# Late loads in larger pieces, a wider output projection and ScalarE centring in a one-core decode block

## The chip, the cores and the metric

The kernel runs on one core of a Trainium2 chip. The metric is the device time of one execution in microseconds (us). TensorE (PE, with its weight loads as PEld), VectorE (DVE), ScalarE (ACT), GpSimd (POOL) and SyncE (SP) are the engines. SP issues nearly all loads; each load is spread over the core's sixteen DMA engines. Every DMA engine works off its share of a queue in order; such a share is called a ring here.

## The reference, cut to what matters

One token (width 512) passes through an attention layer with a cache and then through a small network, with residual additions. x, weights and caches are bf16.

```python
h  = x  + A(layernorm(x))            # attention: 32 query heads, 8 cache heads, 16384 keys, head size 128
h2 = h  + B(layernorm(h))
# A: q = x @ wq; p = softmax(q k^T / sqrt(128)); o = p v; return o(4096) @ wo(4096 x 512)
# B: one token, so the spatial shifts leave nothing of w1, w2:
#    return x + gelu(layernorm(x) @ w3(512 x 1792)) @ w4(1792 x 512)
```

For a sequence of one the shifted slices in B are all padding, so w1 and w2 drop out, and the kernel does not load them. What has to come from memory is 79 MB: the two caches (32 MiB each), wq and wo (4 MiB each), w3 and w4 (1.75 MiB each).

## The kernel before, in words

The program is written as a list of operations per engine. A small planner, `Program.op`, is told what tiles each operation reads and writes, and puts a semaphore wait where another engine or a load has to come first; within an engine the order is that of the source. A load has a semaphore of its own, and an operation that reads a piece of a buffer waits for the load of that piece (`("r", y, n)` are the pieces of key buffer y, `("v", n)` those of the value buffer).

The eight cache heads are taken as four pairs, `j` from 0 to 3. For each pair there are two halves of the keys, loaded into kb[0] and kb[1] (4 MiB each), and the values, loaded into vb (8 MiB). DVE transposes a key half in eight steps into kt (L393), PE makes the scores (L401, 32 products a half in groups of four), and the load of the next pair's half is issued as soon as the transposes have freed the buffer. Then follow the softmax (L412 to L431: a maximum, two small products to spread it, the exponential on ACT, two transposes into pt on DVE, a product that adds up the denominators into one column of A_ps), the values products (L439: sixteen groups of four, each group filling four strips of 32 output rows with 512 columns), and `gather` (L450 to L458), which sums the wanted blocks on DVE and places them in A_ps by one float32 product (L456).

The value load of a pair is issued when the values products of the pair before are done. For pairs 0 to 2 it is one load of 8 MiB. For the last pair it is cut by V3 into the first three quarters and the last quarter, and the products of groups 12 to 15 alone wait for the last quarter.

After the last pair the buffers of keys are used for weights: wo goes into kb[0], as two loads (WO: row blocks 0 to 23 and 24 to 31; a row block is 128 partitions of 512 columns), w3 and w4 into kb[1], w3 as two loads (three of four row blocks, then one) and w4 as four (6, 4, 3 and 1 of 14 row blocks). They are all issued on SP in that order, behind the last value load.

The end of the kernel runs so: DVE takes the reciprocal of the denominators (L484), scales and sums A_ps into the attention output o_b, 128 partitions by 32 columns (L485 to L490). PE adds x by a small product (L491) and then the output projection (L496): for each of 32 row blocks four products of 128 columns, one for each quarter q of the 512 outputs, into strip q of O_ps[0], so that the result lies as 4 strips of 128. `row_sums` (L264 to L275) copies this to hr with its sum, squares it, transposes it to hT, and gets mean and mean square by a float32 product with mean4 (L273). DVE subtracts the mean from the transposed columns (hc, L505). PE multiplies by w3 (L511, sixteen products of 448 columns). The variance and the inverse root (three Newton steps) run on DVE beside it, and once more on POOL for the residual branch, which ends in xsum (L521). ACT applies gelu with the inverse root as its scale (L524, two halves), DVE transposes to hcol (L528), PE multiplies by w4 (L535, four products for each of 14 row blocks), DVE adds xsum (fin, L539), SP stores.

`spin(n)` (L253) puts n products of 128x512 into PE's order, whose result nobody reads.

Of the kernel before, what the change touches and what calls it, by code (L numbers as in the profile page):

```python
# [109 lines left out]
D = 512  # L110
# [6 lines left out]
NCH = D // 128  # L117
FQ = FM // 4
NHC = FM // 128
WO = ((0, 24), (24, 32))  # L120
W3 = ((0, 3), (3, 4))
W4 = ((0, 6), (6, 10), (10, 13), (13, 14))
PAIRS = HKV // 2
V3 = ((0, 3), (3, 4))
RPARTS = 6
QPAD = 4 * 7
QW = QPAD + 128
# [4 lines left out]
def bass_sequential_preLN__gqa_block_cached__mixer_s_mlp__decode_kernel(  # L132
# [13 lines left out]
    with ExitStack() as ctx:  # L146
# [40 lines left out]
        p_sb = sb("p_sb", [128, 1024], BF16)  # L187
        pt = sb("pt", [128, 32, 2, 2, 16], BF16)
        od = sb("od", [128, 128], FP32)
        den = sb("den", [128, 1], FP32)  # L190
        o_m = sb("o_m", [128, 4, 32], FP32)
        o_f = sb("o_f", [128, 32], FP32)
# [27 lines left out]
        def pair_rows(src, j):  # L220
            return src[0, 2 * j:2 * j + 2].rearrange("g (u t) d -> (g u) (t d)", u=64)
# [4 lines left out]
                 also=[("r", y, i) for i in range(1, RPARTS)])  # L226

        def load_values(j):
            src = pair_rows(A_v_cache, j)
            if j < PAIRS - 1:  # L230
                load("v", vb[:, :], src, ("v", 0), also=[("v", 1)])
            else:
                n = 64 * DH
                for i, (lo, hi) in enumerate(V3):
                    load(f"v3{i}", vb[:, lo * n:hi * n], src[:, lo * n:hi * n], ("v", i))


        def dve(fn, r=(), w=(), bank=()):
# [38 lines left out]
        def variance(i):  # L277

            s, S = st[i], ("st", i)

            dve(lambda e: e.scalar_tensor_tensor(s[:, 2:3], s[:, 0:1], s[:, 0:1], s[:, 1:2],
                                                 ALU.mult, ALU.subtract), r=[(S, 0)], w=[(S, 2)])
# [19 lines left out]
        def inverse_root(i, n, by):  # L302
# [7 lines left out]
            for k in range(3):  # L310
# [6 lines left out]


        load("x4", x4[:, :], A_x[0, 0:1, :].rearrange("o (q j) -> (o q) j", q=4), "x4", "ACT")
        load("wq", wq_sb[:, 0:NCH * HQ * DH], A_wq.rearrange("(p k) c -> p (k c)", k=NCH), ("v", 0))  # L320
        load_keys(0, 0)
        load_keys(0, 1)

        dve(lambda e: e.memset(mean4[:, :], 1.0 / (32 * D)), w=["mean4"])
        dve(lambda e: e.memset(ident_f[:, :], 0.0), w=["ident_f"])
        P.op("POOL", lambda e: e.affine_select(out=ident_f[:, :], in_=ident_f[:, :], pattern=[[-1, 128]],  # L326
                                               compare_op=ALU.not_equal, fill=1.0, base=0,
# [10 lines left out]
        seeds(0, (0,))  # L338
        inverse_root(0, 0, dve)
        dve(lambda e: e.tensor_scalar(xn[:, :], hT[:, :, 0], st[0][:, 0:1], st[0][:, 6:7],  # L340
                                      ALU.subtract, ALU.mult),
            r=["hT", (("st", 0), 0), (("st", 0), 6)], w=["xn"])


# [25 lines left out]
        for j, (row, key) in enumerate(rows):  # L370
            for k in range(NCH):
                for g in range(2):
                    at = k * HQ * DH + (2 * j + g) * REP * DH
                    pe(lambda e, row=row, k=k, g=g, at=at: e.matmul(  # L374
                        row[64 * g:64 * g + 64, :], copies(xn[:, k:k + 1], 64), wq_sb[:, at:at + REP * DH],
                        start=(k == 0), stop=(k == NCH - 1)), r=["xn", ("v", 0)], w=[key], bank=[key])
# [32 lines left out]
        def softmax(j):  # L409

            s_all = s_ps[:, :, :].rearrange("p y f -> p (y f)")
            dve(lambda e: e.tensor_reduce(mx[:, :], s_all, AX.X, ALU.max), r=[("s", 0), ("s", 1)], w=["mx"], **both)  # L412
            pe(lambda e: e.matmul(m_ps[0:1, 0:128], mx[:, :], ident_f[:, :], start=True, stop=True),  # L413
               r=["mx", "ident_f"], w=["m"], bank=["mn"])
            dve(lambda e: e.tensor_reduce(nm[:, :, :], m_ps[0:1, 0:128].rearrange("o (g n h) -> o g h n", g=2, h=REP),
                                          AX.X, ALU.max), r=["m"], w=["nm"], bank=["mn"])
            pe(lambda e: e.matmul(n_ps[:, 0:2 * REP], nscale[0:1, :], nm[:, :, :].rearrange("o g h -> o (g h)"),
                                  start=True, stop=True), r=["nm", "nscale"], w=["n"], bank=["mn"])
            dve(lambda e: e.scalar_tensor_tensor(nmh[:, :], n_ps[:, 0:2 * REP], 1.0,  # L419
                                                 maskgh[:, :, :].rearrange("p g h -> p (g h)"), ALU.mult, ALU.mult,  # L420
                                                 accum_out=bias[:, :]), r=["n", "maskgh"], w=["nmh", "bias"],
                bank=["mn"])
            act(lambda e: e.activation(p_sb[:, :], s_all, ACTF.Exp, bias=bias[:, 0:1], scale=float(SCALE),  # L423
                                       accum_out=acc[:, :]),
                r=[("s", 0), ("s", 1), "bias"], w=["p", "acc"], **both)
            for g in range(2):
                dve(lambda e, g=g: e.transpose(pt[64 * g:64 * g + 64, :, :, g, :], p_sb[64 * g:64 * g + 64, :]),  # L427
                    r=["p"], w=["pt"])
            pe(lambda e: e.matmul(A_ps[:, 128:129], zd[:, 96 - 32 * j:224 - 32 * j], acc[:, :],  # L429
                                  start=(j == 0), stop=(j == PAIRS - 1), skip_group_check=True),  # L430
               r=["acc", "zd"], w=["A"], bank=["A"])  # L431

        def values(j):
            tiles = vb[:, :].rearrange("p (x c l d) -> p x l c d", x=4, c=8, l=8)
            for q in range(16):
                for ct in range(4):
                    xl, ch = 2 * q + ct // 2, ct % 2
                    parts = [int(xl // 8 >= V3[1][0])] if j == PAIRS - 1 else [0, 1]
                    pe(lambda e, q=q, ct=ct, xl=xl, ch=ch: e.matmul(  # L439
                        O_ps[j % 2][32 * ct:32 * ct + 32, :], pt[:, xl, ch, :, :].rearrange("p g u -> p (g u)"),  # L440
                        tiles[:, xl // 8, xl % 8, 4 * ch:4 * ch + 4, :], start=(q == 0), stop=(q == 15)),
                       r=[("v", n) for n in parts] + ["pt"], w=[("O", j % 2)], bank=[("O", j % 2)])

        def gather(j):

# [24 lines left out]
            if j < PAIRS - 1:  # L470
                load_values(j + 1)
        act(lambda e: e.activation(scr[0:1, 1:2], mean4[0:1, 0:1], ACTF.Gelu_apprx_tanh), r=["mean4"], w=["scr"])
        for n, (lo, hi) in enumerate(WO):
            load(f"wo{n}", wo_sb[:, lo * D:hi * D], A_wo.rearrange("(p r) c -> p (r c)", p=128)[:, lo * D:hi * D],
                 ("r", 0, n))
        w3_in = B_w3.rearrange("(p k) f -> p k f", p=128)
        for n, (lo, hi) in enumerate(W3):
            load(f"w3{n}", w3_sb[:, lo:hi, :], w3_in[:, lo:hi, :], ("r", 1, n))
# [11 lines left out]
        dve(lambda e: e.tensor_copy(o_b[:, :], o_f[:, :]), r=["o_f"], w=["o_b"])  # L490
        pe(lambda e: e.matmul(O_ps[0][:, 0:128], quarter[:, :, :].rearrange("p q u -> p (q u)"), x4[:, :],  # L491
                              start=True, stop=False, skip_group_check=True),
           r=["quarter", "x4"], w=[("O", 0)], bank=[("O", 0)])
        for r_ in range(32):
            for q in range(4):
                pe(lambda e, r_=r_, q=q: e.matmul(O_ps[0][32 * q:32 * q + 32, 0:128], copies(o_b[:, r_:r_ + 1], 32),  # L496
                                                  wo_sb[:, r_ * D + q * 128:r_ * D + (q + 1) * 128],
                                                  start=False, stop=(r_ == 31), skip_group_check=True),
                   r=["o_b", ("r", 0, piece(WO, r_))], w=[("O", 0)], bank=[("O", 0)])
# [16 lines left out]
        seeds(1, (0, 1))  # L516
        inverse_root(1, 1, dve)
        inverse_root(1, 0, pool)
        pool(lambda e: e.tensor_scalar(xs[:, :], hr[:, :], s[:, 0:1], s[:, 6:7], ALU.subtract, ALU.mult),
            r=["hr", (S, 0), (S, 6)], w=["xs"])  # L520
        pool(lambda e: e.tensor_tensor(xsum[:, :], hr[:, :], xs[:, :], ALU.add), r=["hr", "xs"], w=["xsum"])  # L521
        for n in range(2):
# [6 lines left out]
                hcol[:, lo:hi, :].rearrange("p m u -> p (m u)"),  # L529
                hg[:, :].rearrange("p (i m) -> p m i", m=NHC)[:, lo:hi, :]), r=[("hg", n)], w=[("hcol", n)])  # L530
        for m in range(NHC):
            if m in (W4[1][0], W4[2][0]):
                spin(1)
            for o in range(4):
                pe(lambda e, m=m, o=o: e.matmul(  # L535
                    n_ps[32 * o:32 * o + 32, 0:128], hcol[:, m, :], w4_sb[:, m, o * 128:(o + 1) * 128],
# [38 lines left out]
```

## Time and profile before

| | us |
|---|---|
| median of 3 runs (lowest to highest) | 192.22 (192.14 to 192.45) |
| the profiled execution, its own time | 192.01 |
| its span | 190.7 |
| PE busy, DVE busy, ACT busy, POOL busy | 117.2, 114.8, 8.7, 7.7 |
| DMA: mean rate over the span | 416 GB/s |
| packets' time of the main queue, share of sixteen DMA engines' span | 97.1% |

The page gives for each engine its busy share of the span; for the DMA queues the packets, megabytes and the share of the sixteen engines' time; the chain of work that ended last, followed backwards through what released each step; and groups of instructions by source line with their mean duration and the idle time before them, with what ended it. The timeline shows instructions in order of time: start, length, engine, line, output and inputs, and in brackets the idle time of that engine before it and its releaser. The windows view gives, for stretches of time, the busy time of an engine and the TensorE clock that was granted (1.00 is full speed). The trace also holds each DMA packet with its start, length and size, and the moment at which each of a load's sixteen parts reported its completion.

### The profile page before, as it was taken

The page shows a single profiled execution, that of the slowest core. Times are in us where ns is not written, and L with a number is a line of the kernel's source. Part 1 is how long each engine was busy: PE and PEld are TensorE (multiplying, and loading weights), DVE is VectorE, ACT ScalarE, POOL GpSimd, SP SyncE. Part 2 cuts the span into 40 slices and gives each one's busy share as a digit, 9 for nine tenths or more (in the row PEclk, how much of TensorE's full clock was granted, in tenths as well). Part 3 has the DMA queues.
Part 4 walks back from the last instruction along what each step waited for, and adds up shares of the span by engine and source line. Part 5 has one row for each costly group of instructions (what it writes and reads, how often), then busy time and mean ns, then how long its engine had stood idle before and what let it go on. Part 6 is the DMA issues. An engine that isn't in the chain of part 4 may idle for free.

```text
span 190.7 us, 1877 instructions
## 1 busy us (share of the span) xinstructions
PE 117.2 (61%) x797; PEld 45.6 (24%) x799; DVE 114.8 (60%) x176; ACT 8.7 (5%) x14; POOL 7.7 (4%) x16
## 2 busy tenths in 40 slices
PE   0129098793085598951754979605739996293793
PEld 0114033221031142211221322202213321141632
DVE  7755597984402898945026989550169896605171
ACT  3000000002000000001000000020000000500010
POOL 7100000000000000000000000000000000000052
PEclk9999969999558589995597899975665999659699
DMA  6999999999999999998999999979999998999991
GB/s 227 433 440 440 440 440 442 440 440 430 433 419 426 433 488 440 430 426 351 440 440 440 529 440 430 426 344 412 433 426 423 464 478 351 416 436 406 421 397 62
DMA packets 3191, 79.28 MB, mean 416 GB/s; under 512 B 368, under 2 KB 496, under 8 KB 1008
## 3 DMA queue, kind: packets, MB, share of 16 engines
q1 hardware_dynamic: 3176, 79.17, 97.1%
q8 instruction: 6, 0.10, 0.2%
q14 instruction: 1, 0.01, 0.0%
q10 hardware_dynamic: 8, 0.00, 0.0%
HBM read 79.17 MB, written 0.00 MB: 415 GB/s over the span
## 4 chain that ended last, share of the span: by engine, by line
DMA 77%; DVE 19%; SPq 1%; issue 0%; PE 0%
DMA kb<-in_A_k_cache_dram 63%; DVE kt L393 19%; DMA kb<-in_B_w_dram 14%; SPq L218 1%; PE mn_ps L535 0%; DVE fin L539 0%; SPq L101 0%
## 5 line engine op out<-in xcount | busy, mean ns | idle before, releaser
L401 PE MATMUL s_ps<-kt,qb 128*128 128x512 bf16 x256 | 70.0, 416 | 19.1 <-DVE kt L393 16.6
L393 DVE STREAM_TRANSPOSE kt<-kb 128x1024 int32<-128x1024 int32 x64 | 73.0, 1210 | 11.6 <-DMA kb<-in_A_k_cache_dram 11.6
L401 PEld LDWEIGHTS s_ps<-kt,qb 128*128 128x128 bf16 x256 | 23.3, 104 | 64.8 <-DVE kt L393 38.8
L439 PE MATMUL O_ps<-vb,pt 128*32 128x512 bf16 x256 | 23.6, 550 | 16.8 <-DMA vb<-in_A_v_cache_dram 14.7
L450 DVE TENSOR_SCALAR od<-O_ps,rowc 128x128 f32<-128x128 f32 x4 | 1.4, 351 | 32.7 <-PE O_ps L439 32.7
L439 PEld LDWEIGHTS O_ps<-vb,pt 128*32 128x32 bf16 x256 | 8.9, 132 | 29.9 <-DMA vb<-in_A_v_cache_dram 15.0
L427 DVE STREAM_TRANSPOSE pt<-p_sb 64x1024 bf16<-64x1024 bf16 x8 | 9.9, 1239 | 5.4 <-ACT p_sb L423 5.3
L423 ACT ACTIVATE p_sb<-s_ps,bias 128x1024 bf16<-128x1024 f32 x4 | 4.5, 1114 | 156.7 <-DVE nmh L419 156.7
L412 DVE TENSOR_REDUCE mx<-s_ps 128x1 f32<-128x1024 f32 x4 | 4.9, 1225 | 4.5 <-PE s_ps L401 4.5
L309 POOL TENSOR_SCALAR st<-st 128x1 f32<-128x1 f32 x1 | 0.3, 265 | 177.2 <-DVE st L294 177.2
L374 PE MATMUL O_ps<-vb,xn 128*64 128x512 bf16 x16 | 3.6, 632 | 5.5 <-DMA vb<-in_A_wq_dram 5.5
L456 PE MATMUL A_ps<-od,zo 128*128 128x128 f32 x8 | 2.0, 326 | 6.5 <-DVE od L453 6.5
L429 PE MATMUL A_ps<-acc,zd 128*128 128x1 f32 x8 | 1.9, 311 | 6.3 <-ACT p_sb L423 6.3
L496 PE MATMUL O_ps<-kb,o_b 128*32 128x128 bf16 x128 | 3.3, 282 | 2.4 <-DMA kb<-in_A_wo_dram 2.4
L413 PE MATMUL mn_ps<-ident_f,mx 128*1 128x128 f32 x8 | 1.5, 271 | 5.3 <-DVE mx L412 5.3
L453 DVE SCALAR_TENSOR_TENSOR od<-O_ps,rowc,od 128x128 f32<-128x128 f32 x12 | 4.2, 351 | 0.4
L256 PE MATMUL O_ps<-p_sb,pt 128*128 128x512 bf16 x15 | 4.0, 388 | 0.3 <-issue 0.3
L331 DVE CAST ident<-ident_f 4x4 bf16<-4x4 f32 x1 | 3.8, 3849 | 0.6 <-POOL ident_f L326 0.6
L334 PE MATMUL O_ps<-x,quarter 4*128 4x128 bf16 x1 | 0.3, 282 | 5.8 <-DVE quarter L332 5.8
L378 DVE STREAM_TRANSPOSE qcol<-O_ps 128x256 f32<-128x256 f32 x4 | 1.6, 428 | 3.6 <-PE O_ps L374 3.6
L267 DVE TENSOR_SCALAR_CACHE_REDUCE hr<-O_ps 128x128 f32<-128x128 f32 x2 | 0.6, 292 | 5.1 <-PE O_ps L496 4.7
L496 PEld LDWEIGHTS O_ps<-kb,o_b 128*32 128x32 bf16 x128 | 2.8, 127 | 2.8 <-issue 2.4
(76 smaller groups left out, 47.8 us busy)
## 6 DMA issues: line engine op xcount, KB each, us to landing
kb<-in_A_k_cache_dram SPq DMA_DIRECT2D x8, 4096.0 KB, 29.6
vb<-in_A_v_cache_dram SPq DMA_DIRECT2D x1, 6144.0 KB, 27.3
vb<-in_A_wq_dram SPq DMA_DIRECT2D x1, 4096.0 KB, 12.1
kb<-in_A_wo_dram SPq DMA_DIRECT2D x1, 3072.0 KB, 27.3
vb<-in_A_v_cache_dram SPq DMA_DIRECT2D x1, 2048.0 KB, 31.8
kb<-in_B_w_dram SPq DMA_DIRECT2D x1, 1344.0 KB, 23.6
kb<-in_A_wo_dram SPq DMA_DIRECT2D x1, 1024.0 KB, 29.4
kb<-in_B_w_dram SPq DMA_DIRECT2D x1, 768.0 KB, 25.6
```

The source lines that it names most:

```text
L256: pe(lambda e: e.matmul(O_ps[1][:, :], pt[:, 0:2, :, :, :].rearrange("p n c g u -> p (n c g u)"), p_sb[:, 0:512], start=True, stop=True), ...
L331: dve(lambda e: e.tensor_copy(ident[:, :], ident_f[0:4, 0:4]), r=["ident_f"], w=["ident"])
L374: pe(lambda e, row=row, k=k, g=g, at=at: e.matmul(row[64 * g:64 * g + 64, :], copies(xn[:, k:k + 1], 64), wq_sb[:, at:at + REP * DH], star ...
L393: dve(lambda e, view=view: e.transpose(view(kt), view(kb[y])), r=[("r", y, n) for n in range(RPARTS)], w=[("kt", t)])
L401: pe(lambda e, n=n, c=c: e.matmul(s_ps[:, y, :], qb[:, n, j, QPAD - 4 * c:QW - 4 * c], ktv[:, n // 2, n % 2, :, 8 * c:8 * c + 8, :], start ...
L412: dve(lambda e: e.tensor_reduce(mx[:, :], s_all, AX.X, ALU.max), r=[("s", 0), ("s", 1)], w=["mx"], **both)
L423: act(lambda e: e.activation(p_sb[:, :], s_all, ACTF.Exp, bias=bias[:, 0:1], scale=float(SCALE), accum_out=acc[:, :]), r=[("s", 0), ("s", ...
L427: dve(lambda e, g=g: e.transpose(pt[64 * g:64 * g + 64, :, :, g, :], p_sb[64 * g:64 * g + 64, :]), r=["p"], w=["pt"])
L439: pe(lambda e, q=q, ct=ct, xl=xl, ch=ch: e.matmul(O_ps[j % 2][32 * ct:32 * ct + 32, :], pt[:, xl, ch, :, :].rearrange("p g u -> p (g u)"), ...
L453: dve(lambda e, block=block, c=c: e.scalar_tensor_tensor(od[:, :], block, rowc[:, c:c + 1], od[:, :], ALU.mult, ALU.add), r=[key, "rowc", ...
L456: pe(lambda e: e.matmul(A_ps[:, 0:128], zo[:, 96 - 32 * j:224 - 32 * j], od[:, :], start=False, stop=(j == PAIRS - 1), skip_group_check=True),
L496: pe(lambda e, r_=r_, q=q: e.matmul(O_ps[0][32 * q:32 * q + 32, 0:128], copies(o_b[:, r_:r_ + 1], 32), wo_sb[:, r_ * D + q * 128:r_ * D + ...
```

## The change

- The last pair's values are one load, as for the other pairs.
- wo is loaded as row blocks 0 to 22, then row block 23 in three loads by rows (partitions 0 to 99, 100 to 119, 120 to 127), then blocks 24 to 31. w3 is one load. w4 is three loads (10, 3 and 1 row blocks).
- The projection is 32 products of 512 columns: row block r goes into strip r mod 4 of O_ps[0], so that each strip holds a partial sum of all 512 outputs. DVE copies the 128x512 result to osum in SBUF. Then x is added and the four strips are summed by four float32 products whose stationary operand is 32 copies of row32's first column (it adds the first rows of the four strips), for each quarter of the outputs into its strip of s_ps[:, 1, :], from where `row_sums` goes on.
- The mean is kept with its sign turned, and hc is made by an ACT activation (Identity with the mean as bias) in place of the DVE subtraction.
- The reciprocal of the denominators stands in DVE's order right after the softmax of the last pair.
- The two single spins within the w4 products are gone.

```diff
-WO = ((0, 24), (24, 32))
-W3 = ((0, 3), (3, 4))
-W4 = ((0, 6), (6, 10), (10, 13), (13, 14))
+WO = ((0, 23), (24, 32), (23, 24))
+WO_ROWS = ((0, 100), (100, 120), (120, 128))
+W3 = ((0, 4),)
+W4 = ((0, 10), (10, 13), (13, 14))
-V3 = ((0, 3), (3, 4))
...
-            src = pair_rows(A_v_cache, j)
-            if j < PAIRS - 1:
-                load("v", vb[:, :], src, ("v", 0), also=[("v", 1)])
-            else:
-                n = 64 * DH
-                for i, (lo, hi) in enumerate(V3):
-                    load(f"v3{i}", vb[:, lo * n:hi * n], src[:, lo * n:hi * n], ("v", i))
+            load("v", vb[:, :], pair_rows(A_v_cache, j), "v")
...
-        dve(lambda e: e.memset(mean4[:, :], 1.0 / (32 * D)), w=["mean4"])
+        dve(lambda e: e.memset(mean4[:, :], -1.0 / (32 * D)), w=["mean4"])
...
+            if j == PAIRS - 1:
+                dve(lambda e: e.reciprocal(den[:, :], A_ps[:, 128:129]), r=["A"], w=["den"], bank=["A"])
...
-        for n, (lo, hi) in enumerate(WO):
-            load(f"wo{n}", wo_sb[:, lo * D:hi * D], A_wo.rearrange("(p r) c -> p (r c)", p=128)[:, lo * D:hi * D],
-                 ("r", 0, n))
+        wo_in = A_wo.rearrange("(p r) c -> p (r c)", p=128)
+        for n, (lo, hi) in ((0, WO[0]), (2, WO[2]), (1, WO[1])):
+            for i, (a, b) in enumerate(WO_ROWS if n == 2 else ((0, 128),)):
+                load(f"wo{n + i}", wo_sb[a:b, lo * D:hi * D], wo_in[a:b, lo * D:hi * D], ("r", 0, n + i))
...
-        dve(lambda e: e.reciprocal(den[:, :], A_ps[:, 128:129]), r=["A"], w=["den"], bank=["A"])
...
-        pe(lambda e: e.matmul(O_ps[0][:, 0:128], quarter[:, :, :].rearrange("p q u -> p (q u)"), x4[:, :],
+        for r_ in range(32):
+            q = r_ % 4
+            pe(lambda e, r_=r_, q=q: e.matmul(O_ps[0][32 * q:32 * q + 32, :], copies(o_b[:, r_:r_ + 1], 32),
+                                              wo_sb[:, r_ * D:(r_ + 1) * D], start=(r_ < 4), stop=(r_ >= 28)),
+               r=["o_b"] + [("r", 0, piece(WO, r_) + i) for i in range(3 if r_ == WO[2][0] else 1)], w=[("O", 0)], bank=[("O", 0)])
+        h_ps, hkey = s_ps[:, 1, :], ("s", 1)
+        pe(lambda e: e.matmul(h_ps[:, 0:128], quarter[:, :, :].rearrange("p q u -> p (q u)"), x4[:, :],
                               start=True, stop=False, skip_group_check=True),
-        for r_ in range(32):
-            for q in range(4):
-                pe(lambda e, r_=r_, q=q: e.matmul(O_ps[0][32 * q:32 * q + 32, 0:128], copies(o_b[:, r_:r_ + 1], 32),
-                                                  wo_sb[:, r_ * D + q * 128:r_ * D + (q + 1) * 128],
-                                                  start=False, stop=(r_ == 31), skip_group_check=True),
-                   r=["o_b", ("r", 0, piece(WO, r_))], w=[("O", 0)], bank=[("O", 0)])
+        dve(lambda e: e.tensor_copy(osum[:, :], O_ps[0][:, :]), r=[("O", 0)], w=["osum"], bank=[("O", 0)])
         spin(2)
+        for q in range(4):
+            pe(lambda e, q=q: e.matmul(h_ps[32 * q:32 * q + 32, 0:128], copies(row32[:, 0:1], 32),
+                                       osum[:, q * 128:(q + 1) * 128], start=False, stop=True, skip_group_check=True),
+               r=["osum", "row32"], w=[hkey], bank=[hkey])
...
-        row_sums(1, O_ps[0], ("O", 0))
+        row_sums(1, h_ps, hkey)
         spin(7)
-        dve(lambda e: e.tensor_scalar(hc[:, :, :], hT[:, :, :], s[:, 0:1], None, ALU.subtract),
+        act(lambda e: e.activation(hc[:, :, :], hT[:, :, :], ACTF.Identity, bias=s[:, 0:1], scale=1.0),
...
-            if m in (W4[1][0], W4[2][0]):
-                spin(1)
```

More of the change, by code (lines that the diff above doesn't have):

```diff
@@ L189, in bass_sequential_preLN__gqa_block_cached__mixer_s_mlp__decode_kernel @@
         od = sb("od", [128, 128], FP32)
+        osum = sb("osum", [128, D], FP32)
         den = sb("den", [128, 1], FP32)
@@ L281, in variance @@
             dve(lambda e: e.scalar_tensor_tensor(s[:, 2:3], s[:, 0:1], s[:, 0:1], s[:, 1:2],
-                                                 ALU.mult, ALU.subtract), r=[(S, 0)], w=[(S, 2)])
+                                                 ALU.mult, ALU.add), r=[(S, 0)], w=[(S, 2)])
             dve(lambda e: e.tensor_scalar(s[:, 3:4], s[:, 2:3], 0.0, -1.0, ALU.min, ALU.mult),
@@ L319, in bass_sequential_preLN__gqa_block_cached__mixer_s_mlp__decode_kernel @@
         load("x4", x4[:, :], A_x[0, 0:1, :].rearrange("o (q j) -> (o q) j", q=4), "x4", "ACT")
-        load("wq", wq_sb[:, 0:NCH * HQ * DH], A_wq.rearrange("(p k) c -> p (k c)", k=NCH), ("v", 0))
+        load("wq", wq_sb[:, 0:NCH * HQ * DH], A_wq.rearrange("(p k) c -> p (k c)", k=NCH), "v")
         load_keys(0, 0)
         load_keys(0, 1)
-        dve(lambda e: e.memset(mean4[:, :], 1.0 / (32 * D)), w=["mean4"])
+        dve(lambda e: e.memset(mean4[:, :], -1.0 / (32 * D)), w=["mean4"])
         dve(lambda e: e.memset(ident_f[:, :], 0.0), w=["ident_f"])
@@ L340, in bass_sequential_preLN__gqa_block_cached__mixer_s_mlp__decode_kernel @@
         dve(lambda e: e.tensor_scalar(xn[:, :], hT[:, :, 0], st[0][:, 0:1], st[0][:, 6:7],
-                                      ALU.subtract, ALU.mult),
+                                      ALU.add, ALU.mult),
             r=["hT", (("st", 0), 0), (("st", 0), 6)], w=["xn"])
@@ L375, in bass_sequential_preLN__gqa_block_cached__mixer_s_mlp__decode_kernel @@
                         row[64 * g:64 * g + 64, :], copies(xn[:, k:k + 1], 64), wq_sb[:, at:at + REP * DH],
-                        start=(k == 0), stop=(k == NCH - 1)), r=["xn", ("v", 0)], w=[key], bank=[key])
+                        start=(k == 0), stop=(k == NCH - 1)), r=["xn", "v"], w=[key], bank=[key])
             for b in range(2):
@@ L437, in values @@
                     xl, ch = 2 * q + ct // 2, ct % 2
-                    parts = [int(xl // 8 >= V3[1][0])] if j == PAIRS - 1 else [0, 1]
                     pe(lambda e, q=q, ct=ct, xl=xl, ch=ch: e.matmul(
@@ L441, in values @@
                         tiles[:, xl // 8, xl % 8, 4 * ch:4 * ch + 4, :], start=(q == 0), stop=(q == 15)),
-                       r=[("v", n) for n in parts] + ["pt"], w=[("O", j % 2)], bank=[("O", j % 2)])
+                       r=["v", "pt"], w=[("O", j % 2)], bank=[("O", j % 2)])
         def gather(j):
@@ L490, in bass_sequential_preLN__gqa_block_cached__mixer_s_mlp__decode_kernel @@
         dve(lambda e: e.tensor_copy(o_b[:, :], o_f[:, :]), r=["o_f"], w=["o_b"])
-        pe(lambda e: e.matmul(O_ps[0][:, 0:128], quarter[:, :, :].rearrange("p q u -> p (q u)"), x4[:, :],
-                              start=True, stop=False, skip_group_check=True),
-           r=["quarter", "x4"], w=[("O", 0)], bank=[("O", 0)])
-        for r_ in range(32):
-            for q in range(4):
-                pe(lambda e, r_=r_, q=q: e.matmul(O_ps[0][32 * q:32 * q + 32, 0:128], copies(o_b[:, r_:r_ + 1], 32),
-                                                  wo_sb[:, r_ * D + q * 128:r_ * D + (q + 1) * 128],
-                                                  start=False, stop=(r_ == 31), skip_group_check=True),
-                   r=["o_b", ("r", 0, piece(WO, r_))], w=[("O", 0)], bank=[("O", 0)])
+        for r_ in range(32):
[5 more added lines that the diff above has]
+        pe(lambda e: e.matmul(h_ps[:, 0:128], quarter[:, :, :].rearrange("p q u -> p (q u)"), x4[:, :],
+                              start=True, stop=False, skip_group_check=True),
+           r=["quarter", "x4"], w=[hkey], bank=[hkey])
+        dve(lambda e: e.tensor_copy(osum[:, :], O_ps[0][:, :]), r=[("O", 0)], w=["osum"], bank=[("O", 0)])
         spin(2)
+        for q in range(4):
+            pe(lambda e, q=q: e.matmul(h_ps[32 * q:32 * q + 32, 0:128], copies(row32[:, 0:1], 32),
+                                       osum[:, q * 128:(q + 1) * 128], start=False, stop=True, skip_group_check=True),
+               r=["osum", "row32"], w=[hkey], bank=[hkey])
         s = st[1]
         S = ("st", 1)
-        row_sums(1, O_ps[0], ("O", 0))
+        row_sums(1, h_ps, hkey)
         spin(7)
-        dve(lambda e: e.tensor_scalar(hc[:, :, :], hT[:, :, :], s[:, 0:1], None, ALU.subtract),
+        act(lambda e: e.activation(hc[:, :, :], hT[:, :, :], ACTF.Identity, bias=s[:, 0:1], scale=1.0),
             r=["hT", (S, 0)], w=["hc"])
@@ L518, in bass_sequential_preLN__gqa_block_cached__mixer_s_mlp__decode_kernel @@
         inverse_root(1, 0, pool)
-        pool(lambda e: e.tensor_scalar(xs[:, :], hr[:, :], s[:, 0:1], s[:, 6:7], ALU.subtract, ALU.mult),
+        pool(lambda e: e.tensor_scalar(xs[:, :], hr[:, :], s[:, 0:1], s[:, 6:7], ALU.add, ALU.mult),
             r=["hr", (S, 0), (S, 6)], w=["xs"])
```

## The prediction

> **What bounds the kernel now.** I read the queue part of the page first, then the chain of waits in order of time, then the timeline of the last 25 us, then the windows of the PE clock.
>
> ```profile
> DMA  6999999999999999998999999979999998999991
> q1 hardware_dynamic: 3176, 79.17, 97.1%
> q8 instruction: 6, 0.10, 0.2%
> ```
>
> The sixteen DMA rings are full from start to end: 79 MB have to come in, and the queue rows show no pause in which an engine held them up. The second queue row matters too: six fetches of PE instructions, 16 KB each, ride on the same rings (a ring is one of the sixteen DMA engines' share of a queue).
>
> ```profile
> 161.12 26.94 DMA kb<-in_B_w_dram
> 188.06 0.04 issue
> 188.10 0.59 PE mn_ps L535 x16
> ...
> 188.72 0.29 DVE fin L539
> ```
>
> The chain (start, length, what) ends: last weights land, 16 products, the final addition, the store. So the end is the **slowest ring**. The trace's sixteen completion counts of the very last load (one row of w4 per partition) come at 186.39 to 186.96 for ten rings and 187.62 to 188.38 for six. At the first load all sixteen lay within 0.43 us; one more ring drops back by 0.75 to 1.2 us after each instruction fetch (PE's at 43.8, 80.0, 116.3, 153.4 and 180.7 us, and another engine's of 8 KB at 30.4; PE's sixth, at 186.3, met a ring that was done). Six rings are late because each carried a fetch; the end is 188.38 + 0.34 = 188.72 where fin starts (0.34: count to product 0.05, four products and their drain 0.23, to DVE 0.06).
>
> Behind the loads the engines run a chain of their own:
>
> ```profile
> 166.99 5.49 PE L439 MATMUL O_ps<-vb,pt 128*32 128x512 bf16 x64 [2.04 <-DVE pt L427]
> ...
> 172.53 0.35 DVE L450 TENSOR_SCALAR od<-O_ps,rowc 128x128 f32<-128x128 f32 x1 [5.69 <-PE O_ps L439]
> ...
> 175.61 0.18 DVE L490 CAST o_b<-o_f 128x32 bf16<-128x32 f32 x1
> ...
> 177.00 2.23 PE L496 MATMUL O_ps<-kb,o_b 128*32 128x128 bf16 x96 [2.26 <-DMA kb<-in_A_wo_dram]
> ...
> 180.50 0.29 DVE L267 TENSOR_SCALAR_CACHE_REDUCE hr<-O_ps 128x128 f32<-128x128 f32 x1 [4.71 <-PE O_ps L496]
> ...
> 184.74 0.86 ACT L524 ACTIVATE hg<-s_ps,st 128x224 bf16<-128x224 f32 x2 [18.91 <-DVE st L314]
> ```
>
> The first bracket is the one to see: the last values products waited for pt (DVE), not for vb. Their first three quarters of V had landed at 164.66 and the last quarter only at 169.55, used by the last four of sixteen groups. Then the projection waited for wo (176.87, 179.36): this chain had slack.
>
> **The change part by part.**
>
> *The last V load in one piece.* All 64 values products now wait for the whole load. In the earlier pairs V is one load, and there the products start 0.04 us after its last ring. So they start at 169.52 instead of 166.99: **2.5 us of slack are spent.** On the loads' side, one descriptor costs 7.7 ns beside its bytes (32 KB take 1216 ns, 3 KB 121 ns, so 0.0369 ns per byte), eight and a count make 0.068 us per load and ring; one load fewer is -0.07.
>
> *How long the values take.* Groups of four products step by 0.427 us while the clock is at 0.5 and by 0.216 at 1.0. The clock changes at multiples of 3.413 us, and the windows show by what:
>
> ```profile
> 129.83:133.24 3.41, 2.52 (x24) 0.50 0.94 404
> 133.24:136.66 3.42, 3.42 (x36) 0.50 1.02 441
> 136.66:140.07 3.41, 1.09 (x14) 1.00 1.07 461
> ...
> 167.38:170.79 3.41, 3.41 (x37) 0.50 0.99 425
> 170.79:174.20 3.41, 1.79 (x33) 1.00 1.03 440
> 174.20:177.62 3.42, 1.16 (x48) 1.00 0.93 388
> ```
>
> (columns: window, length, PE busy, clock granted, DMA, GB/s). Busy 2.52 of 3.41 did not raise the clock, 2.91 and more did; 1.79 kept it, 1.16 dropped it for the next, and around 1.5 it went either way (the windows from 17.19 and 58.15). With the grid of this execution, the values from 169.52 fill too little of the window to 170.79, so the clock rises only at 174.20: eleven slow groups, five fast, drain 0.16, done at 175.44 (5.92 us; the four pairs took 6.12, 5.49, 6.55 and 5.49).
>
> *To o_b.* From 172.48 to 175.79 is 3.31; the reciprocal moves ahead beside the values products (0.17 + 0.04; DVE is idle there): 3.10, so 178.54.
>
> *Projection.* 128 products of 128 columns become 32 of 512: eight groups, 7 x 0.216 + 0.38 = 1.89 on the fast clock, 3.6 on the slow. The window 174.20 to 177.62 now holds 1.2 of the values and 0.5 of L456: 1.7 of 3.41, like the one that kept the clock. Start 178.60, end 180.49; wo is in by 179.0.
>
> *New steps.* The copy of 128x512 from PSUM lies between the 128x128 step (0.29) and the 128x1024 maximum (1.23): by their slope 0.69; the two spins hide under it. Four float32 products: one alone took 0.38 (L413, two passes 0.11 apart); 0.42 if the four overlap, 1.15 if they queue in full; I take 0.72, passes in order. With 0.05 to 0.06 per handover, hr starts at 182.06, 1.56 late.
>
> *Centred columns by ScalarE.* DVE loses 0.20 (181.81 to 182.01). ACT was idle; its 128 columns come to 0.41 from 0.49 at 224 and 1.11 at 1024, and end before the seven spins free PE (2.55 after hr): free. Should it want a new table, 1.28 (the load at L472) would be added; the instruction order has none.
>
> *From hr to fin.* ACT's L524 began 4.24 after hr, now 4.04; the second half of hcol 1.62 later; 28 products and drain 0.61; handover 0.06: 6.33. POOL's xsum ends 6.28 after hr, just hidden. fin at **188.39**. By then w3 (183.4) and w4 to row 10 (186.6) are in; the spins taken out only waited.
>
> *Loads on the late rings.* Where a ring gets none of the 100, 20 and 8 rows, it carries 8 KB less (-0.30) and seven loads instead of ten (v, w3, w4 each one fewer: -0.20). A load of 128 rows shows sixteen completions, one of 4 rows four, so equal shares: 100 and 20 rows divide by ten, 8 by eight, and six rings are left out. That is -0.50: fin at **188.22**. If the rows spread evenly after all, it is -0.20. The Trainium skill, "DMA: Bandwidth & Descriptors", section "Why a DMA increments its semaphore by 16 and not by 1", says the same: the largest divisor up to 16, 100 rows on ten, on the lowest-numbered rings. By it the spared ones would be the six highest; no row here numbers a ring.
>
> *SP.* Three more issues near 150 (0.43 each) and two fewer near 160; the rings had some 25 us of work queued then, so nothing waits.
>
> *Sum.* fin starts at the later of 188.22 and 188.39 against 188.72: -0.33 here, -0.50 where the clock grid lies better, -0.06 at the worst grid that still keeps the clock; I take **-0.4**. The profiled execution took 192.01 (span 190.7 and 1.3 around it), 0.21 under the median 192.22; on the median's scale 191.8.
>
> **The rivals.**
>
> *Cold projection (slower).* The place is the window in which the values end. If under some 45% of it is busy, the projection runs at 0.5: 3.3 to 3.6 instead of 1.89, behind late values. With the pattern of the third pair (values 6.55, clock dropped at 140.07): 169.52 + 6.55 + 3.16 + 3.4 + 1.57 + 6.33 = 190.5, +1.8; with others +1.2 to +1.9, so 193.4 to 194.1. For it: two of three earlier pairs, which start at V's landing as the last now does, lost the clock in this way. Against it: the grid of this execution. Moving the grid through all positions with these bounds, 36% of them lose the clock. Whether the grid moves from run to run one trace can't show; I give 0.33. The Trainium skill, "TensorE: Matmul & The Clock Gate", Part 1, calls the window free-running, not reset by a kernel's start: by that the chance would be those 36% for each run.
>
> *The spared rings are not the late ones.* Then a late ring gets up to 5 KB more (+0.19) and saves 0.09 in packets: +0.1, fin at 188.82, 192.3, no change. For it: no row says which rings the fetches took. Against: each fetch hit a ring not hit before, so they walk through the rings, and there are six late and six spared. 0.17.
>
> *The new steps cost more* (the products in full, a copy above 0.69, a wait after ACT): +0.7 on 188.39, 192.7 or so. 0.05.
>
> **How the numbers follow.** Forecast 0.45 (-0.5 to -0.06: 191.6 to 192.15, with 0.2 of spread 191.4 to 192.3), cold projection 0.33, wrong rings 0.17, dearer steps 0.05. Over 0.2% is 0.38 us, about what a measurement of this kernel tells from no change. The forecast splits at 191.84: 0.33 faster, 0.12 same. Same 0.12 + 0.17 = 0.29; slower 0.33 + 0.05 = 0.38. Cases of both signs hold most of the chance, so the range runs from 191.4 to 193.9; the likeliest case alone has 191.4 to 192.3.
>
> **What the profile after would show.** Values starting near 169.5 and waiting for vb; clock 1.0 at the projection from 178.6 (wrong: 0.5, hr near 184); hr near 182, fin near 188.3; completions of the last load within about 1.0 us of each other, the latest near 187.9 (wrong: still 188.4 or later); one fetch fewer; hc on ACT near 0.4 with no table load. I am wrong if values start before 169, or if the loads end late although the engines wait for nothing.

## The result and the profile after

The changed kernel takes 192.87 us (median of 21 runs, 192.15 to 195.03); the kernel before, beside it, 192.09 (21 runs, 191.88 to 192.51). The ratio is 1.0045, 95% interval 1.0031 to 1.0058: 0.6 to 1.1 us slower (0.8 by the medians), where 0.4 us faster was forecast. The medians hide what happened to the spread: 0.6 us before, 2.9 us after. Seven of the 21 runs lie at 192.15 to 192.45, and these had a mean granted clock of 0.837 to 0.848; the other fourteen go up to 195.03, with 0.813 to 0.836. The profiled execution is one of the fourteen: 193.09, span 191.8.

From the page of the changed kernel, the row for what moved and the rows of its queues:

```profile
DMA  6999999999999999999999999989999999899990
q1 hardware_dynamic: 2900, 79.17, 96.7%
q8 instruction: 5, 0.08, 0.2%
```

The same bytes; one instruction fetch fewer, as forecast. But the chain that ended last is another one. From its answer in order of time (start, length, what), the end:

```profile
178.94 3.28 PE O_ps L490 x32
182.23 0.70 DVE osum L497
...
182.98 0.47 PE s_ps L500 x8
183.47 0.31 DVE hr L262 x2
...
187.50 0.50 ACT hg L526
188.03 0.59 DVE hcol L530
...
188.66 1.09 PE mn_ps L535 x56
189.78 0.29 DVE fin L539
```

Before, a load ended the kernel (`DMA kb<-in_B_w_dram` up to 188.06). Now the engines do: the projection takes 3.28 us, and when the w4 products begin, nothing waits for a load any more. fin starts at 189.78 instead of 188.72; that +1.06 is nearly all of the 1.08 between the two profiled executions (193.09 and 192.01). Why 3.28, the timeline says, and two windows (their columns: window, length, PE busy and instructions, clock granted, DMA share, GB/s):

```profile
169.51 6.25 PE L435 MATMUL O_ps<-vb,pt 128*32 128x512 bf16 x64 [4.74 <-DMA vb<-in_A_v_cache_dram]
...
178.94 3.24 PE L490 MATMUL O_ps<-kb,o_b 128*32 128x512 bf16 x32 [1.06 <-DVE o_b L486]
...
184.77 0.40 ACT L507 ACTIVATE hc<-hT,st 128x128 bf16<-128x128 f32 x1 [18.93 <-DVE st L270]
```
```profile
174.85:178.27 3.42, 1.40 (x18) 1.00 1.02 360
```
```profile
178.27:181.68 3.41, 2.75 (x28) 0.50 0.99 417
```

The bracket of the values products now names the load (`DMA vb`), where it named pt before. They end at 175.76, so the window from 174.85 is busy for 1.40 of 3.41 us only, and the next one, in which the projection runs, gets half the clock.

The loads did not end sooner either. The sixteen completions of the last load come at 186.75 to 187.29 for ten rings and at 188.04, 188.05, 188.21, 188.90, 188.91 and 188.92 for six: the latest 0.54 **later** than before (188.38). For this reason alone an execution with a good clock gains nothing: the seven lowest runs lie 0.1 to 0.4 us above the median before.

### The profile page after: what moved, and what is told of

Its sections match the earlier page's. It is cut to its first block, busy times and chain, and to the rows that moved or that the text cites. A ratio compares the mean times of both kernels' runs of the same rounds, so it can differ in the third digit from the quotient of the medians.

```text
span 191.8 us, 1700 instructions
## 1 busy us (share of the span) xinstructions
PE 117.7 (61%) x708; PEld 44.1 (23%) x709; DVE 115.3 (60%) x176; ACT 9.1 (5%) x15; POOL 7.4 (4%) x16
## 4 chain that ended last, share of the span: by engine, by line
DMA 76%; PE 18%; DVE 4%; issue 1%; ACT 0%; SPq 0%; ACTq 0%
DMA vb<-in_A_v_cache_dram 69%; PE O_ps L435 12%; DMA vb<-in_A_wq_dram 6%; PE O_ps L369 2%; PE O_ps L490 2%; PE s_ps L369 1%; PE mn_ps L535 1%; DVE od L449 1%; DVE st L307 0%; DVE osum L497 0%; DVE hcol L530 0%; PE A_ps L452 0%; ACT hg L526 0%; PE s_ps L500 0%; PE mn_ps L268 0%
## 5 line engine op out<-in xcount | busy, mean ns | idle before, releaser
L490 PE MATMUL O_ps<-kb,o_b 128*32 128x512 bf16 x32 | 3.2, 579 | 1.1 <-DVE o_b L486 1.1
L251 PE MATMUL O_ps<-p_sb,pt 128*128 128x512 bf16 x14 | 3.5, 379 | 0.2 <-issue 0.2
L452 PEld LDWEIGHTS A_ps<-od,zo 128*128 128x128 f32 x8 | 1.2, 188 | 8.5 <-DVE od L449 8.5
L424 PEld LDWEIGHTS A_ps<-acc,zd 128*128 128x128 f32 x8 | 1.6, 250 | 6.6 <-ACT p_sb L418 6.6
```

The lines of the kernel that those rows point to most:

```text
L251: pe(lambda e: e.matmul(O_ps[1][:, :], pt[:, 0:2, :, :, :].rearrange("p n c g u -> p (n c g u)"), p_sb[:, 0:512], start=True, stop=True), ...
```

## The experiments

Two questions: what holds the loads back, and what spreads the runs. The first theory was the rival of the prediction made larger (rows on late rings), with V's late landing as the source of the spread. A low mean clock alone does not make a run long: beside the first of these kernels the kernel before had clocks of 0.818 to 0.848 in 35 runs, all within 191.84 to 192.58, and its runs at 0.818 took 192.01, 192.08 and 192.35. The profile before has a stretch at half clock in the projection too (177.62 to 181.03) and still ends on a load: its slack hides the lost clock. What counts is how much slack a version has left. Of each version one execution was profiled, so what the profiles say of the clock holds for that execution, and for the other runs only time and mean clock are known. Every kernel was timed beside the kernel before on the same chip; the kernel before had medians of 192.11 to 192.12 in all three sittings.

**V cut again.** The changed kernel with

```diff
-            load("v", vb[:, :], pair_rows(A_v_cache, j), "v")
+            # in words: one load for j < PAIRS - 1, as now; for the last pair three quarters,
+            # then one quarter, and the values products wait for their part
```

> The changed kernel with the last V load cut again into three quarters and one quarter. Theory (V's late landing makes the chain meet the clock's grid): values start near 167.0 again, hr 1 to 3 us earlier than the 183.47 of the changed kernel's profile, the projection's clock no longer decides the end, the runs lie within 0.8 us of each other, and the end is set by the rings: median 192.3 to 192.6. Rival (the wide projection, the copy and the float32 products carry the loss whatever V does): the spread of 2.9 us stays and the median stays near 192.9.

Measured: 192.69 (192.16 to 195.08). Values start at 167.13 as expected, and nine of twelve runs lie at 192.16 to 193.0, but three at 194.8 to 195.1. The profiled execution (192.52) is bound by loads, last completion 188.83. The spread stays as large as it was, so V's late start is at most one of its sources: **the theory fell in half.** Three of twelve runs above 193.05 against ten of 21 are too few to say by themselves that it is one; "V whole alone" below says it.

**Without the loads by rows.** The changed kernel with

```diff
-WO = ((0, 23), (24, 32), (23, 24))
-WO_ROWS = ((0, 100), (100, 120), (120, 128))
+WO = ((0, 24), (24, 32))
```

> The changed kernel with wo loaded as 24 and 8 row blocks, without the three loads by rows. Theory (the rows were put on rings that are late themselves, so their 13 rows cost these rings some 0.5 us): the last completion of the last load comes at 188.2 to 188.4 instead of 188.92; the fastest runs come to 191.7 to 191.9 instead of 192.15, and the slow ones stay near 193 to 195, since the clock is untouched; median 192.5. Rival (the rows relieve the late rings, as forecast): the last completion moves later and every run gets slower by 0.3 or more.

Measured: 192.01, in two groups: seven runs at 191.66 to 192.08, five at 193.56 to 193.72. The last completion is at 188.09. The expected median was 192.5; seven of twelve runs fell into the lower group, so it came out lower. The lower group moved by 0.4 to 0.5 against the changed kernel's, as the theory had it. With the rows gone, the lower group lies 0.2 under the kernel before. In its profile (191.72) the clock is at 1.0 from 172.29 on, hr starts at 181.23, and fin at 188.43 comes 0.34 after the last completion: with the clock held the chain is hidden behind the loads.

**Both undone.** The two edits above together; what is left of the change is the wide projection, the w3 and w4 loads, ACT's centring, the early reciprocal and the missing single spins.

> The changed kernel with the cut of V restored and without the loads by rows: what is left is the wide projection, w3 and w4 in fewer loads, ACT's centring and the reciprocal. Theory: both losses are gone, runs within 0.7 us, median 191.8 to 192.0, 0.1 to 0.2 under the kernel before for two loads fewer per ring at 0.068 us. Rival (the new steps cost more): above 192.3.

Measured: 192.17, eight runs at 191.77 to 192.20, four at 194.16 to 194.96. The runs spread even with V cut and without the rows, where runs within 0.7 us had been expected. In its profile (192.04) the projection ran at half clock, starting at 176.93 for wo, and the chain just met the loads' end:

```profile
176.93 3.60 PE L496 MATMUL O_ps<-kb,o_b 128*32 128x512 bf16 x32 [1.81 <-DMA kb<-in_A_wo_dram]
...
182.37 0.29 DVE L268 TENSOR_SCALAR_CACHE_REDUCE hr<-s_ps 128x128 f32<-128x128 f32 x1 [1.09 <-PE s_ps L506]
...
188.71 0.29 DVE L545 TENSOR_TENSOR fin<-xsum,mn_ps 128x128 bf16<-128x128 f32 x1 [0.68 <-PE mn_ps L541]
```

fin waits for products that no load delayed (188.71, where the last completion at 188.16 alone would give 188.50): there is no slack left, and any further loss of clock in this chain lengthens the kernel.

**Idle products ahead of the values.** The changed kernel with

```diff
             softmax(j)
+            if j == PAIRS - 1:
+                spin(6)
             values(j)
```

> The changed kernel with six idle products of 128x512 on PE between the last softmax and the last values products, in the time in which PE waits for V. Theory (the clock decides): the clock rises while or before the values run, values take 3.6 to 5 us instead of 6.25, hr comes before 182.4 in nearly all runs, and the runs above 193 disappear; median 192.3 to 192.5, the rings' bound with the rows in. Rival (the clock is not what spreads the runs): as many runs above 193 as without.

Measured: 192.71 (192.42 to 194.56). Ten of twelve runs lie within 192.42 to 193.0, two at 193.96 and 194.56. Fewer runs are high, but they have not gone, and the median lies above the 192.3 to 192.5 that had been expected. Its profile (192.67) shows the next place where the clock is lost:

```profile
169.71 4.82 PE L435 MATMUL O_ps<-vb,pt 128*32 128x512 bf16 x64
...
180.11 0.61 PE L492 MATMUL O_ps<-kb,o_b 128*32 128x512 bf16 x8 [0.92 <-DMA kb<-in_A_wo_dram]
...
183.15 2.97 PE L251 MATMUL O_ps<-p_sb,pt 128*128 128x512 bf16 x7
...
186.04 0.94 PE L515 MATMUL s_ps<-kb,hc 128*32 128x448 bf16 x16
```
```profile
178.98:182.39 3.41, 1.94 (x23) 1.00 1.00 419
```

Values take 4.82 instead of 6.25. But the seven spins behind hr took 2.97 instead of the 1.67 of the changed kernel's profile: the clock fell at 182.39, after a window with 1.94 busy us, whose longest pause (0.92) was the wait for wo. PE could begin the w3 products only when its idle work was done, 1.3 us later than with spins at full clock.

**The rows alone.** The kernel before with nothing but the three loads by rows:

```diff
-WO = ((0, 24), (24, 32))
+WO = ((0, 23), (24, 32), (23, 24))
+WO_ROWS = ((0, 100), (100, 120), (120, 128))
```

> The kernel before with one part of the change alone: row block 23 of wo by loads of 100, 20 and 8 rows. Theory (rows on late rings cost about 0.5 us of DMA time, the clock is not concerned): every run shifts together, median 192.5 to 192.7, spread as before, the last completion 0.5 later than 188.38. Rival (the rows hurt only with the other parts): within 0.2 of 192.12.

Measured: 192.71, ten of eleven runs at 192.29 to 193.08, one at 193.73; +0.60. In its profile (192.98, above the median) the last completion is at 189.32 (188.38 before), and the chain's end is a load's again:

```profile
163.11 25.87 DMA kb<-in_B_w_dram
188.98 0.04 issue
189.03 0.60 PE mn_ps L537 x16
...
189.65 0.29 DVE fin L541
```

The other profiles say the same of the last completion: 188.09 to 188.49 in the eight whose wo comes in two loads and that add no load of their own, 188.79 to 189.32 in the four with loads by rows. **That the loads by rows make the end later is shown** by taking them out and by putting them in alone.

**The narrow projection.** "Both undone" with the 128 products of 128 columns in place of the wide projection, its copy and its float32 products:

```diff
-        # in words: for each r_ one product of 512 columns; copy to osum; four float32 products
+        # in words: for each r_ four products of 128 columns into O_ps[0], as before the change
...
-        row_sums(1, h_ps, hkey)
+        row_sums(1, O_ps[0], ("O", 0))
```

> The kernel before with w3 as one load, w4 as three, ACT's centring and the early reciprocal, and nothing else: V cut, 128 narrow projection products, no loads by rows. Theory (the wide projection streams the same 4096 column groups and adds a copy and float32 products of 1.3 us, in which PE loses its clock; without it the slow runs vanish): all runs between 191.6 and 192.4, median 191.9 to 192.0. Rival (the slow runs come from ACT or the missing spins in the w4 products): runs above 193.5 stay, as in the version with the wide projection.

Measured: 192.27, all eleven runs within 192.14 to 192.44. No run above: **the wide projection with its copy is the second source of the spread**, ACT and the missing spins are not. None of eleven against four of twelve is not many; that one of twelve against five of twelve goes the same way with V whole (below) supports it. The profile shows the slack that is regained:

```profile
180.85 0.29 DVE L268 TENSOR_SCALAR_CACHE_REDUCE hr<-O_ps 128x128 f32<-128x128 f32 x1 [4.66 <-PE O_ps L499]
```

hr starts here 1.5 us earlier than in "Both undone" (182.37). The median is not below the kernel before, as had been expected of fewer loads (ratio 1.0008, interval 0.9999 to 1.0017); what they saved is not to be seen at this size. Its profile contains seven spins of 3.15 us at half clock as well, and it did not matter: fin at 188.78, 0.34 after the last completion.

**No spins around the w3 products.** "Both undone" with

```diff
-        spin(7)
...
-        spin(6)
```

> The changed kernel with V cut again, no loads by rows, and without the seven and six spins around the w3 products (two spins before the float32 products stay). Theory (in the slow runs the clock falls in the gap of the copy, and thirteen spins at half clock, 2.97 for seven instead of 1.67, then hold PE): the runs at 194.2 to 195.0 move to 193.0 or below, the others stay near 192.1. Rival (the slow runs come from the projection itself at half clock): they stay above 194.

Measured: 192.72 (191.95 to 192.96); five runs at 191.95 to 192.24, seven at 192.70 to 192.96. The runs above 194 are gone, as the theory had it: the top of the spread goes with the idle products. That they hold PE at half clock in the high runs themselves is argued, since no such run was profiled. Seven runs now have a lower mean clock (0.796 to 0.807) at a price of 0.6 to 0.8 instead of 2 to 3 us.

**Which rings are late.** The kernel before with loads of 1, 2, ... 16 rows of 1 KB into a tile that nothing uses (they add work; the time is not comparable):

```diff
+        for n in range(1, 17):
+            load(f"t{n}", probe[0:n, n, :], A_wq[0:n, 0:512], ("probe", n))
```

> The kernel before with sixteen loads of 1 KB rows into a scratch tile ahead of w4, of 1, 2, 3 ... 16 rows, which nothing uses; the load of n rows reaches n rings. The completions of load n are those of load n-1 plus one, so the added one tells whether ring n-1 is late. Theory (three of the late rings lie among the first eight): late completions (0.7 to 1.4 us behind) join at three or more loads of 1 to 8 rows, two near the end. Rival (the late rings are the last six): they join only from 11 rows on.

Measured, in one profiled execution: the completions of the first loads, from the trace (us; one early completion of each load, at the time of its issue, is left out):

```
1 row   182.74
2 rows  182.45 182.93
3 rows  182.58 182.66 183.11
4 rows  182.79 182.87 183.30 183.98
5 rows  182.23 182.97 183.05 183.50 184.16
6 rows  182.46 183.15 183.23 183.68 184.35 185.22
```

Each list is the one above, some 0.2 later, and one more entry; that entry is the new ring's. By this the new ring is on time (182.2 to 183.1) for 1, 2, 3, 5, 8, 9 and 13 to 16 rows, and late for 4 (183.98), 6 (185.22), 7 (184.44), 10 (184.93), 11 (184.29) and 12 rows (183.78). So, counted from 0 in the order in which they join, rings 3, 5, 6, 9, 10 and 11 are late in this execution: a load of 8 rows reaches three of them, those of 20 and 100 rows, on ten rings, four, and the six spared rings contain two. The changed kernel's own trace fits: its 8-row load completes at 175.62 to 176.21 on five rings and at 177.20, 177.98 and 177.99 on three. But two other profiles with the same loads have another set: in "V cut again" and "Idle products" the 8-row load meets only two late rings (177.54 and 177.94; 177.55 and 177.97), and so do the loads of 20 and 100 rows. Which rings are late is thus not fixed, and the end is late with two as well (188.83 and 188.79). The Trainium skill, "DMA: Bandwidth & Descriptors", section "Why a DMA increments its semaphore by 16 and not by 1", says that a load on fewer than sixteen rings uses the lowest-numbered ones. The nested lists agree in so far as each load reaches the rings of the one before and one more.

The 0.2 between the lists is a second finding: one more load with a single 1 KB row costs its ring 0.2 us, although its packet of 1 KB takes 0.046 and the packet of its completion 0.009. The changed kernel's loads of 20 and 8 rows, two rows and one on a ring, show 0.2 each too (177.55, 177.77, 177.98 on a late ring).

**Small loads without the uneven share.** The kernel before with row block 23 by columns instead of rows:

```diff
-WO = ((0, 24), (24, 32))
+WO = ((0, 23), (24, 32), (23, 24))
+WO_COLS = ((0, 176), (176, 344), (344, 512))
```

> The kernel before with row block 23 of wo as three loads by columns (176, 168 and 168 columns of all 128 rows): as many loads as by rows, but the same share on every ring. If the number of small loads is the cost, the median is 192.5 or more, like the 192.71 with the loads by rows; if the uneven share is, it is within 0.25 of 192.11. From the tiny loads (0.2 us each on a ring for one row) the count should carry a part: 192.3.

Measured: 192.40 (192.18 to 192.66), +0.29 (interval 0.1 to 0.5). As many loads with equal shares cost about half of the 0.60, so the uneven share is not the whole of it. The split is not clean: the columns also cut each row of 1 KB into three packets, and a ring's 24 packets of 21 ns take 0.50 us where eight of 46 ns take 0.37. How much the number of loads costs by itself stays open.

**V whole alone.** The kernel before with the last pair's values as one load:

```diff
-                for i, (lo, hi) in enumerate(V3):
-                    load(f"v3{i}", vb[:, lo * n:hi * n], src[:, lo * n:hi * n], ("v", i))
+            load("v", vb[:, :], src, ("v", 0), also=[("v", 1)])
```

> The kernel before with one part of the change alone: the last pair's values as one load. Theory (2.5 us of slack go, and the narrow projection leaves enough when the clock holds): most runs stay within 192.0 to 192.5, and a fifth to a third of them, those with a cold projection and spins at half clock, come to 192.8 to 194. Rival (V whole is enough for the whole loss): the median moves to 192.6 or more. Rival (V costs nothing without the wide projection): no run above 192.8.

Measured: 192.53; six runs at 191.90 to 192.13, six at 192.92 to 193.86. The lower half lies 0.1 under the median of the kernel before, about what one load less was forecast to save (0.07); the other half has a lower mean clock (0.813 to 0.831 against 0.837 to 0.848). A fifth to a third had been expected: half did. Since no run of the kernel before lies above 192.62 beside it, **V's late start is a source of the spread.**

**V whole with the narrow projection.** The changed kernel with two edits from above, the 128 narrow products and wo in two loads:

> The changed kernel with the narrow projection of 128 products and without the loads by rows: V whole, w3 and w4 in fewer loads, ACT's centring, early reciprocal. Theory (the loss beside the rows is the wide projection's copy and float32 products, 1.3 us of chain, on top of V's 2.5): clearly fewer slow runs than the 5 of 12 with the wide projection, none above 193.2, median 192.0 to 192.2. Rival (V's late start alone makes the slow runs): 4 to 5 of 12 above 193.3.

Measured: 192.22, eleven of twelve runs at 192.07 to 192.46, one at 193.08. One run in twelve is up, against five with the wide projection ("Without the loads by rows"). Against V whole alone it has 0.4 us more slack (the early reciprocal and ACT's centring took 0.2 each off the chain) and fewer loads and spins; which of these saved the other five runs was not taken apart.

**A version that keeps the clock.** The changed kernel without the rows and with

```diff
             softmax(j)
+            if j == PAIRS - 1:
+                spin(6)
...
-        spin(7)
+        spin(4)
...
-        spin(6)
+        spin(3)
```

> The changed kernel without the loads by rows, with six spins ahead of the last values products, and four and three spins in place of seven and six around the w3 products. Theory (clock and spins make the slow runs): values on the fast clock for most of their length, no run above 193.2, ten of twelve between 191.6 and 192.3, median 191.8 to 192.0, under the kernel before. Rival (the slow runs have another source): 4 or 5 of 12 above 193.3 as without.

Measured: **191.79, all eleven runs within 191.64 to 192.19**; ratio to the kernel before 0.9989, interval 0.9980 to 0.9997. It beats the kernel before by 0.2 us (0.06 to 0.4), and the changed one, which was timed at another time, by 1.1 (medians). Its profile (191.78):

```profile
169.74 4.82 PE L434 MATMUL O_ps<-vb,pt 128*32 128x512 bf16 x64
...
177.72 1.48 PE L490 MATMUL O_ps<-kb,o_b 128*32 128x512 bf16 x24 [1.06 <-DVE o_b L486]
179.48 0.61 PE L490 MATMUL O_ps<-kb,o_b 128*32 128x512 bf16 x8 [0.28 <-DMA kb<-in_A_wo_dram]
...
182.32 1.81 PE L250 MATMUL O_ps<-p_sb,pt 128*128 128x512 bf16 x4
184.06 1.68 PE L513 MATMUL s_ps<-kb,hc 128*32 128x448 bf16 x16
...
188.49 0.29 DVE L539 TENSOR_TENSOR fin<-xsum,mn_ps 128x128 bf16<-128x128 f32 x1 [1.11 <-PE mn_ps L535]
```
```profile
178.99:182.41 3.42, 2.12 (x25) 1.00 1.01 419
```

The clock holds through the projection, which waits for wo again (`DMA kb`). It falls at 182.41 even here, after a window with 2.12 busy us: four spins take 1.81 and the w3 products 1.68, and yet the loads decide the end (last completion 188.16, fin 0.33 later). With fewer spins the lost clock did no harm in this execution. The run changes two things at once, spins ahead of the values and fewer behind hr, and does not tell which of them removed the high runs.

## Why the prediction was wrong, point by point

**The step that failed first: -0.50 on the late rings.** The forecast let the six spared rings be the six late ones, with the argument that fetches walk through neighbouring rings. They are not: in every profile with these loads at least two late rings take the 8, 20 and 100 rows, four in the changed kernel's own for the 20 and 100. In the one that numbers the rings the late ones are 3, 5, 6, 9, 10 and 11, which are not neighbours, and two of the six are spared. The last completion came 0.54 later (188.92 instead of 188.38), where 0.50 earlier was forecast. The rival "the spared rings are not the late ones" had the mechanism, but its price, +0.1, was mis-sized: the rows alone cost 0.60. It counted 13 rows at the price of descriptors in a long load. In the changed kernel's trace the three loads put 1.05 us on a late ring that takes all of them (176.93 before them, 177.98 after), where eight rows in a long load take 0.30 by the prediction's own price; less the 0.20 for three loads fewer, that is the 0.54 to within 0.01.

**The step that failed second: the window in which the values end.** The working took the grid of the profile before and 1.7 busy us in that window, and found the clock held. The profile after has its windows 0.65 us later (171.44 where 170.79 was), the window is busy for 1.40, and the clock falls. Nor was 1.7 a safe figure: a window of 1.50 in the profile before kept the clock, while those of 1.94 and 2.12 shown above lost it, so the busy time alone does not tell. The price for that rival was nearly right in the profile (projection 3.24, forecast 3.3 to 3.6; fin +1.06, forecast +1.2 to +1.9). Its frequency had been worked out as 36%. Ten of the changed kernel's 21 runs are at 193.07 or more, six of twelve with V whole alone and five of twelve without the rows are up: nearer to half, though so few runs do not exclude 36%. (Four more of the 21, at 192.72 to 192.87, are no higher than the rows alone can make them.) The Trainium skill, "TensorE: Matmul & The Clock Gate", Part 1, calls the window free-running. The profiles agree in so far as two kernels have two grids; no kernel was profiled twice, so that the grid moves from run to run is not shown directly. The rival ended at +1.9, and the highest runs are at +2.8 and +2.9. It left out the thirteen spins at half clock; that they make the difference is argued from "No spins around the w3 products", as none of the highest runs was profiled.

The measured median lies in the stated range only because this rival had widened it; the likeliest case alone had the sign wrong.

**What held.** Values start at 169.51 (forecast 169.52); from their end to o_b 3.12 (3.10); copy 0.69 (0.69); ACT 0.40 without a table load (0.41); hr to fin 6.31 (6.33). The float32 products take 0.42, not 0.72: the four overlap. So the chain was sized well wherever the clock did not enter: 2.5 us spent on V, 1.2 on copy, products and handovers, 0.4 given back by reciprocal and centring. With the clock held it stays hidden behind the loads (the profile without the rows). What the chain's sum then hung on was the clock, and that was read from one execution.

**Where the gain went.** The lower groups of V whole alone and of the version without rows lie 0.1 and 0.2 us under the kernel before, but a lower group is the better part of the runs; the narrow projection with fewer w3 and w4 loads, with all its runs, shows no gain (+0.16). A gain from fewer loads is shown only for the version that keeps the clock, as a whole: 0.2 us. The loads by rows cost 0.4 to 0.6; the upper groups, with the lower clock, lie 1.5 to 3 us above the lower ones of the same version (without the rows, both undone). The wide projection itself saves no PE time: at the full clock the narrow products step by 0.056 us per group of four for 128 columns, the wide ones by 0.216 for 512, nearly the same rate, and 32 row blocks took 1.97 us narrow (V whole with the narrow projection) and 1.48 + 0.61 wide (the version that keeps the clock).

## What to carry to other kernels

A kernel bound by loads has slack in its engines only as far as the clock they run at: before spending it, work out the chain once at half clock, with every idle product in it, and not only for the window positions of one profile. Do not build on guesses about which DMA rings are late: loads of 1, 2, 3 ... rows tell it for one execution, and here the set differed between profiles, so that equal shares are the safe choice. Count each small load at its own price, as measured among full queues. Idle products that keep the clock up ahead of a wait help; behind one they hold the engine for nearly twice their length when the clock is lost (2.97 or 3.15 us instead of 1.67), so use as few as cover the wait.

## What the runs showed of the hardware that had not been expected

- In the profile before, six rings complete the last load 0.7 to 1.4 us behind the slowest of the other ten, and one more had dropped back after each instruction fetch of 16 KB (a packet of 1.0 to 1.1 us). That the fetches cause it is concluded from this order in time; no run moved a fetch. The late rings were 3, 5, 6, 9, 10 and 11 in one execution, and another set in two others.
- A load with one row of 1 KB per ring takes 0.2 us of the ring's time among full queues, though its packets take 0.046 and 0.009.
- One program (the version without rows) had two groups of times 1.5 us apart, and their mean PE clocks differ too: 191.66 to 192.08 with 0.836 to 0.839, 193.56 to 193.72 with 0.814 to 0.823.
- A window of 3.41 us in which PE was busy for 1.94 or 2.12 was followed by half clock, one with 1.50 by full clock.
- Four float32 products into four strips of 32 rows overlap: 0.42 for all, 0.38 for one alone.
